# A gated linear attention feeding an expert layer: another order table for the same operations

## The chip, the cores and the metric

The kernel runs on one core of one Trainium2 chip. The metric is device time in microseconds (us), lower is better. The profiler's span, from the first to the last instruction of one execution, is a little shorter than the device time, because what lies around the program is not in it.

## The reference, cut to what matters

```
a = a * min(|a|, 0.999) / (|a| + 1e-6)            # complex a = a_re + i*a_im, per head, step, channel
for t in range(768):                              # 4 batches, 8 heads, channels of 48
    S = a[t] (*) S + outer(k[t], v[t])            # complex state 48 x 48
    y[t] = q[t] . Re(S)
x  = y with the heads side by side                # 4 x 768 x 384
xn = (x - mean(x)) / sqrt(var(x) + 1e-6) * g_ln
out = x + relu(xn @ w_ch1) @ w_ch2                # 384 -> 1536 -> 384
```

All inputs and the output are 32-bit floats. The loop over time is not run step by step. Over a chunk of 128 steps it is a masked attention: keys and queries are scaled by the running product of the decays and turned by the running phase, and a 48 x 48 state per head is carried from chunk to chunk.

## The kernel before

The 24 chunks (four batches of six) are worked in twelve pairs, P = 0 to 11; three pairs make a batch. Pair 0 alone is cut into two halves of four heads. The program is a graph of named operations with a hand-written table, PLAN, that gives the order in which they are emitted. A token such as `wl.1:G@r2.2.0` names the operation, its engine (P TensorE, V VectorE, A ScalarE, G GpSimd, S the SyncE queue that issues DMAs), for some a PSUM bank, and behind `@` an operation that it must follow. Each engine works strictly down its own list, and so does SyncE: what stands behind a waiting instruction waits too. `Graph.run` only asserts that the order is legal. What the table decides is therefore the order on each queue and, for many operations, which engine does them. Line numbers here are those of the profile of the kernel before.

One pair goes through these operations (P is the pair, n = 2P or 2P+1 the chunk):

- Loads on SyncE: `are`, `aim` (L444), `k`, `q`, `vf` (L403). A queue slot is used again only when the DMA eight issues before has landed.
- Decays, on ScalarE and VectorE: `ln` (L447), `iv` (L449), `r` = aim/are (L291), `r2`, `u` (L461), `l` (L465), `lc` (L468), then `dec` on TensorE (L476), a running sum over time, and `e`, `en` (L480), its exponentials.
- Phases: `th`, the arctangent (L484); `ph` on TensorE (L491, L495), the running sum with the carry `car` of the pair before; `sin` (L513); `qt` (L520), which adds a quarter turn in PSUM for pairs 0 to 3; `cos` (L524, L536). `tab` loads the function table for logarithms or for sines on ScalarE (L774).
- `ke`, `qe` scale keys and queries, `ks`, `qs` turn them (all L291, on VectorE or GpSimd); `v` converts the values (L413, L411).
- The turned keys and queries are needed transposed, as `ksT` and `qsT`. Either TensorE transposes them (`kT`, `qT`, L592) and VectorE or ScalarE copies the PSUM bank out (L288, L286), or one DMA transpose on SyncE does both (L597).
- `am` (L615) is scores, `atm` the mask (L291), `gm` and `G` (L643) the state, `dps` and `decc` (L572, L288) its decay, `y` (L665, L668) the output of the chunk, `x` its copy, `bn` the mean and variance, `xtr`, `xT` (L686) its transpose.
- `mm1` (L719), `relu` (L730, L732), `mm2` (L740), `ot` (L754, or `oa` and L752) and the store `st` (L760) are the feed-forward part.

Besides these, once per run: six weight loads `wl` issued by GpSimd, which convert to 16 bits on the way (L363 for `w_ch1`: wl.0 to wl.2; L365 for `w_ch2`: wl.3 to wl.5); `gln` and `wgc`, the norm's gain; `wp` (L383) and nine `wc` on VectorE (L387), which fold the gain and the mean into `w_ch1`, and which every `mm1` needs; small constants on GpSimd (`ue`, `uth`, `pick`, `ident`, `mask`, `pad`, `zdec`, `car0`, `qrow`); and fillers `warm` on TensorE (L769), multiplies whose result nobody reads.

In the order of before, GpSimd makes the constants first and issues wl.1 and wl.0 behind `r2.2.0`, wl.2 behind `qs.0.0.0` and wl.3, wl.4, wl.5 behind `v.1`. SyncE asks for the `are` and `aim` of pairs 0 to 2 first, then for `k.0.0`, `k.0.1` and `gln`, then for the rest.

Of the kernel before, what the change touches and what calls it, by code (L numbers as in the profile page):

```python
# [54 lines left out]
sin.0.0:A0 ke.0.1.0:G@lc.2.0 car.0.1:V1 sin.0.1:A1 qe.0.1.0:V qt.0.0:P0 th.2.0:A qt.0.1:P1 ph.1.0:P6
ks.0.1.1:V cos.0.0:A0 qs.0.1.1:V ks.0.0.1:V cos.0.1:A1 wp.1:P2 ks.0.0.0:V qs.0.0.1:V qs.0.0.0:V dec.2.0:P4
wc.1.0:V2 wl.2:G@qs.0.0.0 warm.69:P3 warm.70:P0 wc.1.2:V2 tab.log.2:A ln.3.0:A qs.0.1.0:G wp.0:P3 wc.1.1:V2
en.2.0:A4 ks.0.1.0:G wc.0.1:V3 qT.0:P0 iv.3.0:A wc.0.0:V3 v.0:G kT.0:P1 e.2.0:A4 wc.0.2:V3 warm.71:P2
pad.qs.1:G qsT.0:A0 qT.1:P4 ksT.0:V1 r.3.0:G vf.1.1:S kT.1:P5 qsT.1:V4 car.1.0:A6 am.0:P2 ksT.1:V5 vf.1.0:S
ph.2.0:P0 atm.0:V2 qe.1.0.1:G am.1:P4 q.2.1:S tab.trig.3:A sin.1.0:A6 ke.1.0.0:G atm.1:V4 gm.0:P2 sin.2.0:A0  # L60
are.4.0:S qt.1.0:P6 ke.1.0.1:G y.0:P3 cos.1.0:A6 qt.2.0:P0 G.0:V2 wp.2:P4 ks.1.0.1:V x.0:A3 q.2.0:S cos.2.0:A0
y.1:P5 ks.1.0.0:V xtr.0:P3 qs.1.0.1:V gm.1:P2 aim.4.0:S x.1:A5 kT.3:P6 qs.1.0.0:V th.3.0:A kT.2:P5 G.1:V2
v.1:G@qs.1.0.0 xtr.1:P7 xT.0:A3 qT.2:P0 ksT.2:V5 k.2.0:S xT.1:A7 qT.3:P1 wl.3:G ksT.3:V6 mm1.0.0.1:P2 qsT.3:V1
mm1.0.0.0:P2 r2.3.0:G qsT.2:V0 tab.log.4:A ln.4.0:A am.3:P6 wc.2.1:V4 mm1.0.1.1:P0 relu.0.0:A2 wl.4:G atm.3:V6
mm1.0.1.0:P0 u.3.0:A gm.2:P5 qe.2.0.1:G wc.2.2:V4 am.2:P2 relu.0.1:A0 ph.3.0:P6 wl.5:G wc.2.0:V4 iv.4.0:A
G.2:V5 mm1.0.2.1:P0 qe.2.0.0:G atm.2:V2 y.3:P4 r.4.0:G mm1.0.2.0:P0 car.3.0:V6 y.2:P2 x.3:V4 tab.trig.5:A
sin.3.0:A6 mm2.0.0:P3 x.2:V2 relu.0.2:A0 xtr.3:P4 qs.2.0.0:G bn.1:V qt.3.0:P6 gm.3:P5 mm2.1.0:P2 xT.3:V4
cos.3.0:A6 k.2.1:S xtr.2:P4 mm2.0.1:P3 r2.4.0:A pad.ks.2:G xT.2:V4 q.3.0:S G.3:V5 qs.2.0.1:G mm2.1.1:P2
th.4.0:A bn.3:V mm1.1.0.1:P0 vf.2.0:S bn.2:V mm1.1.2.1:P6 bn.0:V are.6.0:S rstd.1:G mm1.1.2.0:P6 tab.log.6:A
u.4.0:A l.3.0:V mm2.0.2:P3 rstd.0:G k.3.1:S relu.1.2:A6 mm1.1.0.0:P0 l.4.0:V mm1.1.1.1:P4 relu.1.0:A0 q.3.1:S  # L70
lc.3.0:V ke.2.0.1:V mm1.1.1.0:P4 ke.2.0.0:V are.5.0:S dec.3.0:P6 relu.1.1:A4 ks.2.0.1:V mm2.2.0:P0 lc.4.0:V
ks.2.0.0:V ln.6.0:A mm2.2.1:P0 k.3.0:S ot.0:V3 e.3.0:A6 mm2.2.2:P0 vf.2.1:S en.3.0:A6 qT.4:P1 qe.3.0.0:V
kT.4:P3 qe.3.0.1:V iv.6.0:A st.0:S dec.4.0:P4 qs.3.0.1:V aim.5.0:S qsT.4:A1 mm2.1.2:P2 qs.3.0.0:V ksT.4:V3
dps.3:P6 ke.3.0.1:G@qs.3.0.0 en.4.0:A4 qT.5:P7 vf.3.1:S ot.2:V0 mm2.3.0:P1 ln.5.0:A ke.3.0.0:G qsT.5:V7
q.4.0:S qT.6:P0 e.4.0:A4 decc.3:V6 ks.3.0.1:V kT.5:P3 oa.1:A2 am.4:P6 qsT.6:V0 vf.3.0:S v.2:G@ks.3.0.1
ph.4.0:P4 iv.5.0:A ksT.5:V3 ks.3.0.0:G k.4.0:S atm.4:V6 gm.4:P0 car.4.0:A4 am.5:P2 G.4:A0 aim.6.0:S mm2.3.1:P1
atm.5:V2 r.5.0:G kT.6:P0 qT.7:P6 q.4.1:S y.5:P7 tab.trig.7:A sin.4.0:A4 qsT.7:V6 kT.7:P2 ot.1:G k.4.1:S x.5:A7
y.4:P3 ksT.7:V2 th.5.0:A mm2.3.2:P1 v.3:G x.4:V3 vf.4.0:S abs.4.0:A4 dps.4:P6 ksT.6:V0 qe.4.0.0:G xtr.4:P7
am.7:P2 r2.5.0:A xT.4:V7 q.5.0:S xtr.5:P0 decc.4:V6 am.6:P4 r.6.0:G ot.3:V1 xT.5:A0 ph.5.0:P6 cos.4.0:A
vf.4.1:S atm.6:V4 mm1.2.1.1:P0 sin.5.0:A6 are.7.0:S ke.4.0.0:G atm.7:V2 y.6:P4 mm1.2.1.0:P0 abs.5.0:A6  # L80
ke.4.0.1:G gm.6:P5 x.6:A4 are.8.0:S mm1.2.2.0:P2 G.6:V5 cos.5.0:A qe.4.0.1:G xtr.6:P4 relu.2.1:V0 y.7:P6
gm.7:P5 q.5.1:S ks.4.0.1:G x.7:A6 mm1.2.2.1:P2 bn.4:V r2.6.0:A xtr.7:P0 mm1.2.0.1:P6 vf.5.0:S xT.7:V0
relu.2.2:A2 xT.6:V4 mm1.2.0.0:P6 qs.4.0.0:G G.7:V5 st.1:S th.6.0:A bn.7:V mm1.3.0.0:P0 k.5.0:S relu.2.0:V6
mm1.3.1.0:P2 ks.4.0.0:G aim.7.0:S mm1.3.2.1:P4 bn.5:V mm1.3.2.0:P4 tab.log.8:A u.5.0:A bn.6:V rstd.2:G
mm1.3.1.1:P2 u.6.0:A qs.4.0.1:V mm2.5.0:P6 l.5.0:V relu.3.2:A4 qsT.9:S mm2.4.0:P7 mm1.3.0.1:P0 lc.5.0:V
relu.3.1:A2 l.6.0:V ksT.8:S mm2.4.1:P7 ln.7.0:A relu.3.0:V0 dec.5.0:P4 vf.5.1:S mm2.4.2:P7 e.5.0:A4 q.6.1:S
lc.6.0:V v.4:V mm2.5.1:P6 en.5.0:A4 st.3:S qe.5.0.1:V dec.6.0:P2 ot.4:V7 k.5.1:S iv.7.0:A mm2.6.0:P0 en.6.0:A2
r.7.0:G k.6.1:S qT.8:P1 kT.9:P7 ln.8.0:A qsT.8:V1 mm2.5.2:P6 aim.8.0:S e.6.0:A2 ksT.9:V7 am.8:P4 qe.5.0.0:G
r2.7.0:A mm2.7.0:P1 atm.8:V4 st.4:S gm.8:P7 rstd.3:A qs.5.0.0:G st.2:S am.9:P2 u.7.0:A G.8:V7 aim.9.0:S
mm2.6.1:P0 atm.9:V2 ph.6.0:P4 ke.5.0.0:G k.6.0:S qs.5.0.1:V y.9:P2 tab.trig.9:A th.7.0:A gm.9:P7 l.7.0:V  # L90
y.8:P3 q.6.0:S mm2.7.1:P1 abs.6.0:A4 x.9:V2 ke.5.0.1:G@l.7.0 mm2.6.2:P0 are.9.0:S car.6.0:A4 G.9:V7 sin.6.0:A4
mm2.7.2:P1 x.8:V3 qe.6.0.1:V oa.6:A0 qT.11:P7 vf.6.0:S bn.8:V xtr.8:P2 xtr.9:P3 ph.7.0:P4 lc.7.0:V xT.9:A3
q.7.1:S xT.8:V2 cos.6.0:A ks.5.0.0:V mm1.4.1.1:P2 abs.7.0:V4 vf.6.1:S ke.6.0.1:G@ks.5.0.0 car.7.0:A4
mm1.4.1.0:P2 sin.7.0:A4 ks.5.0.1:V dps.6:P0 qsT.10:S oa.7:A1 v.5:V mm1.4.0.1:P4 relu.4.1:A2 ke.6.0.0:V
mm1.4.0.0:P4 qsT.11:V7 ot.6:G@ke.6.0.0 k.7.1:S kT.11:P1 relu.4.0:V4 mm1.4.2.0:P2 ks.6.0.0:G k.7.0:S
mm1.4.2.1:P2 decc.6:V0 tab.log.10:A ln.9.0:A ksT.11:V1 mm2.8.0:P7 q.7.0:S relu.4.2:A2 ot.5:V6 qe.6.0.0:G
kT.10:P0 bn.9:V am.11:P4 k.8.1:S iv.8.0:A qs.6.0.0:G mm2.9.0:P6 ksT.10:V0 rstd.4:A st.6:S dec.7.0:P2 atm.11:V4
iv.9.0:A st.5:S mm2.8.1:P7 k.8.0:S e.7.0:A2 r.8.0:V gm.10:P0 mm2.9.1:P6 en.7.0:A2 ks.6.0.1:V am.10:P4 G.10:A0
qs.6.0.1:V ksT.13:S mm2.8.2:P7 r.9.0:V qT.13:P0 mm2.9.2:P6 atm.10:V4 qsT.12:S ke.7.0.0:G@r.9.0 tab.trig.11:A
# [706 lines left out]
```

## Time and profile before

| | |
|---|---|
| Device time, median of three runs | 192.42 us (191.69 to 193.0) |
| Span of the profiled execution | 190.8 us |
| Device time of that execution | not listed by itself; the median is 1.6 us over the span |
| TensorE busy | 174.8 us |
| VectorE, ScalarE, GpSimd busy | 154.8, 157.3, 109.9 us |
| TensorE, mean granted clock | 0.987 of full speed |
| DMA transposes of `ksT`, `qsT` | 12 and 10 |
| TensorE transposes `kT`, `qT` | 12 and 14 groups of eight |
| Fillers | 72 |

How to read it: a busy share tells how long an engine had something in it, and TensorE's ends are modelled, so the share alone doesn't say that it is the bound. The timeline by engine tells when an operation started and what it waited for. The chain is the path that ended last, followed back. SPq and POOLq stand for the issuing of DMAs by SyncE and GpSimd; "to landing" is the time from a DMA's issue until its semaphore says that all of it has arrived.

### The profile page before, as it was taken

The page shows a single profiled execution, that of the slowest core. Times are in us where ns is not written, and L with a number is a line of the kernel's source. Part 1 is how long each engine was busy: PE and PEld are TensorE (multiplying, and loading weights), DVE is VectorE, ACT ScalarE, POOL GpSimd, SP SyncE. Part 2 cuts the span into 40 slices and gives each one's busy share as a digit, 9 for nine tenths or more (in the row PEclk, how much of TensorE's full clock was granted, in tenths as well). Part 3 has the DMA queues.
Part 4 walks back from the last instruction along what each step waited for, and adds up shares of the span by engine and source line. Part 5 has one row for each costly group of instructions (what it writes and reads, how often), then busy time and mean ns, then how long its engine had stood idle before and what let it go on. Part 6 is the DMA issues. An engine that isn't in the chain of part 4 may idle for free.

```text
span 190.8 us, 5173 instructions
## 1 busy us (share of the span) xinstructions
PE 174.8 (92%) x2061; PEld 134.5 (70%) x2061; DVE 154.8 (81%) x283; ACT 157.3 (82%) x217; POOL 109.9 (58%) x128
## 2 busy tenths in 40 slices
PE   5758777999999999999899999999999999999990
...
DVE  0397879998979999969979899798998898596422
...
PEclk9978999999999999999999999999999999999998
DMA  5999999899999999699989999987999999995132
GB/s 140 290 226 220 204 207 192 204 193 200 203 240 201 228 236 219 115 221 255 246 147 240 150 241 272 188 190 144 227 205 145 185 186 172 239 121 164 45 124 84
DMA packets 129768, 36.78 MB, mean 193 GB/s; under 512 B 123984, under 2 KB 129744, under 8 KB 129744
## 3 DMA queue, kind: packets, MB, share of 16 engines
...
## 4 chain that ended last, share of the span: by engine, by line
PE 50%; DMA 15%; DVE 9%; ACT 6%; POOL 6%; SPq 6%; issue 4%; POOLq 0%; DVEq 0%; ACTq 0%
PE banks L740 17%; PE banks L719 14%; DMA aim<-in_a_im_dram 5%; DMA w2b<-in_moe_w_ch_dram 4%; PE banks L592 4%; SPq L403 3%; PE banks L615 3%; PE banks L495 3%; DMA are<-in_a_re_dram 2%; PE banks L476 2%; DMA qsT<-qs 2%; DVE atm L291 2%; DMA q<-in_q_dram 2%; POOL r L291 2%; PE banks L665 2%
## 5 line engine op out<-in xcount | busy, mean ns | idle before, releaser
L740 PE MATMUL banks<-w2b,h 128*128 128x384 bf16 x288 | 55.3, 326 | 0.3 <-DMA w2b<-in_moe_w_ch_dram 0.3
L719 PE MATMUL banks<-xT,w1b 128*128 128x256 bf16 x432 | 51.3, 273 | 0.9 <-ACT trig L513 0.9
L719 PEld LDWEIGHTS <-w1b 128*128 128x128 bf16 x432 | 41.4, 98 | 7.3 <-issue 0.8
L740 PEld LDWEIGHTS <-h 128*128 128x128 bf16 x288 | 25.8, 97 | 13.5 <-issue 0.4
L291 DVE TENSOR_TENSOR atm<-banks,mask 128x1024 bf16<-128x1024 f32 x24 | 28.8, 1218 | 3.6 <-PE banks L615 3.5
L730 ACT ACTIVATE h<-banks 128x1024 bf16<-128x1024 f32 x26 | 26.0, 1019 | 5.7 <-PE banks L719 4.4
L291 POOL TENSOR_TENSOR ke<-k,en 128x384 bf16<-128x384 f32 x19 | 17.2, 916 | 16.8 <-DVE qs L291 5.8
L774 ACT ACT_TABLE_LOAD x19 | 24.4, 1283 | 1.1 <-PEq L790 0.8
L291 POOL TENSOR_TENSOR ks<-ke,trig 128x768 bf16<-128x768 bf16 (+1 forms) x12 | 18.9, 1583 | 6.6 <-DVE qs L291 2.0
L752 POOL TENSOR_TENSOR ot<-ot,x 128x384 f32<-128x384 f32 x7 | 6.4, 916 | 18.2 <-ACT ot L745 15.9
L291 POOL TENSOR_TENSOR qs<-qe,trig 128x768 bf16<-128x768 bf16 (+1 forms) x10 | 15.7, 1569 | 0.3
L754 DVE SCALAR_TENSOR_TENSOR ot<-banks,rstd,x 128x384 f32<-128x384 f32 x17 | 10.3, 610 | 6.8 <-ACT h L730 3.5
L615 PE MATMUL banks<-qsT,ksT 128*128 128x128 bf16 x192 | 14.6, 219 | 1.1 <-DVE ksT L288 0.9
L291 POOL TENSOR_TENSOR qe<-q,e 128x384 bf16<-128x384 f32 x14 | 12.7, 918 | 4.2 <-ACT trig L513 3.4
L615 PEld LDWEIGHTS <-ksT 128*128 128x128 bf16 x192 | 12.0, 98 | 3.2 <-DVE ksT L288 1.0
L291 POOL TENSOR_TENSOR r<-aim,are 128x768 f16<-128x768 f32 x6 | 10.9, 1816 | 5.5 <-ACT are L449 5.4
L476 PE MATMUL banks<-l,u_e 128*128 128x384 f16 (+1 forms) x52 | 10.9, 342 | 3.5 <-DVE l L468 3.4
L732 DVE TENSOR_SCALAR h<-banks 128x1024 bf16<-128x1024 f32 x10 | 12.1, 1216 | 2.0 <-PE banks L719 2.0
L678 DVE BATCH_NORM_STATS2 stats<-x 128x6 f32<-128x384 bf16 x24 | 13.1, 547 | 0.0
L769 PE MATMUL banks<-u_e 128*128 128x256 f16 x72 | 11.1, 312 | 2.2 <-POOL u_e L325 2.2
L447 ACT ACTIVATE w<-are 128x768 f32<-128x768 f32 (+1 forms) x13 | 10.1, 794 | 3.4 <-DMA are<-in_a_re_dram 3.3
L665 PE MATMUL banks<-v,atm 128*128 128x48 bf16 x192 | 12.1, 183 | 0.1
...
## 6 DMA issues: line engine op xcount, KB each, us to landing
...
are<-in_a_re_dram SPq DMA_DIRECT2D x11, 384.0 KB, 4.6
aim<-in_a_im_dram SPq DMA_DIRECT2D x11, 384.0 KB, 5.0
w1b<-in_moe_w_ch_dram POOLq DMA_DIRECT2D x3, 384.0 KB, 7.0
w2b<-in_moe_w_ch_dram POOLq DMA_DIRECT2D x3, 384.0 KB, 7.7
```

The source lines that it names most:

```text
L291: {"DVE": nc.vector, "POOL": nc.gpsimd}[eng(name)].tensor_tensor(**kw)
L476: nc.tensor.matmul(heads(ps[:, c]), lhsT=u_e[:, c, j], rhs=step(T("l", P), j), start=(j == 0), stop=(j == R - 1))
L615: nc.tensor.matmul(ps[:, h], lhsT=T("ksT", n)[:, h], rhs=T("qsT", n)[:, h], start=True, stop=True)
L665: nc.tensor.matmul(ps[:, h], lhsT=T("atm", n)[:, h], rhs=T("v", P)[:, c, h], start=True, stop=nfirst)
L678: nc.vector.bn_stats(out=T("stats", n), in_=T("x", n))
L719: nc.tensor.matmul(ps[:, jj], lhsT=w1b[:, dc, ts(gi * JG + jj, C)], rhs=T("xT", P)[:, dc].rearrange("p c t -> p (c t)"), start=(dc == 0), ...
L730: act(out=dst, in_=src, func=AF.Relu)
L732: nc.vector.tensor_scalar(out=dst, in0=src, scalar1=0.0, scalar2=None, op0=ALU.max)
L740: nc.tensor.matmul(bank(f"o.{n}")[:, 0:DM], lhsT=T("h", P)[:, j, ts(c, C)], rhs=w2b[:, j], start=(j == 0), stop=(j == NJ - 1))
L754: nc.vector.scalar_tensor_tensor(out=T("ot", n), in0=bank(f"o.{n}")[:, 0:DM], scalar=T("rstd", P)[:, ds(c, 1)], in1=T("x", n), op0=ALU.mul ...
L769: g.add(f"warm.{i}", lambda i=i: nc.tensor.matmul(bank(f"warm.{i}")[:, 0:256], lhsT=u_e[:, 0, 0], rhs=u_e[:, 1].rearrange("p j t -> p (j t ...
L774: g.add(f"tab.{nm}.{i}", lambda tab=tab: nc.scalar.preload_act_table_set(tab))
```

## The change

The table PLAN is replaced by another one and the number of fillers goes from 72 to 93. No operation is defined otherwise. The other line numbers shift by one.

- Weights: GpSimd issues wl.0 as its first instruction, wl.1 after seven constants, wl.2 after `r2.0.0`, `r2.0.1` and five more constants, then wl.5 and wl.4, and wl.3 a little later, all before its first `v` or `ke`.
- SyncE: the loads of pair 0's `k`, `q`, `vf` stand further back. `k.0.1` and `k.0.0` are the 14th and 15th DMA (9th and 8th before), `vf.0.0` the 23rd (17th before); `gln` is the 6th, and `vf.1.0` stands before `are.2.0`.
- Pair 0: `th` and `ph` come before `l`, `lc` and `dec`; the table loads of ScalarE are moved accordingly, 19 as before.
- VectorE: all of `ks.0` and `qs.0` and all nine `wc` come before `ksT.0`, and `r.3.0` too. Before, GpSimd did one `ke`, one `ks` and one `qs` of pair 0 and three `wc` came later.
- DMA transposes: 29 (11 `ksT`, 18 `qsT`) in place of 22. TensorE transposes: 13 `kT` and 6 `qT` in place of 12 and 14.
- Engines of other operations: `relu` 23 on ScalarE and 13 on VectorE (26 and 10 before), `v` none on VectorE (4 before), `r` 8 on GpSimd (6), `ks` 9 on GpSimd (12), and so on.
- The order of the feed-forward parts among the later pairs is another.
- Fillers: 37 before the first `ph`, 15 before `dec.0.0`, 5 around `wp.1`, 36 before `wp.2`.

The start of the two tables (about the first sixth of each; the rest differs in the same manner):

```diff
-ue:G are.0.0:S are.0.1:S aim.0.1:S uth:V are.1.0:S warm.0:P0 warm.1:P0 qrow:G@uth aim.0.0:S warm.2:P0
-warm.3:P0 pad.qs.2:G@uth warm.4:P0 aim.1.0:S warm.5:P0 zdec:G pad.ks.0:G warm.6:P0 warm.7:P0 warm.8:P0
...
-lc.0.1:V ln.2.0:A lc.0.0:V dec.0.1:P0 l.1.0:V q.1.0:S dec.0.0:P1 en.0.1:A0 warm.42:P2 warm.43:P2 iv.2.0:A
-warm.44:P4 lc.1.0:V q.0.1:S wgc:V dec.1.0:P2 en.0.0:A1 q.0.0:S r.2.0:V warm.45:P4 e.0.1:A0 warm.46:P4
-warm.47:P4 e.1.0:A2 warm.48:P4 warm.49:P4 warm.50:P4 vf.0.1:S ke.0.0.0:V e.0.0:A1 dps.1:P4 r2.2.0:V en.1.0:A2
-dps.0:P5 vf.0.0:S decc.1:V4 wl.1:G@r2.2.0 warm.51:P0 warm.52:P0 u.2.0:A decc.0:V5 warm.53:P0 warm.54:P0
-warm.55:P0 aim.3.0:S warm.56:P0 wl.0:G warm.57:P0 warm.58:P0 l.2.0:V warm.59:P0 warm.60:P0 warm.61:P0
...
+are.0.0:S tab.log.0:A ln.0.0:A iv.0.0:A are.0.1:S aim.0.1:S aim.0.0:S are.1.0:S gln:S r.0.0:V wl.0:G ln.0.1:A
+iv.0.1:A r.0.1:V ue:G uth:V one:G cmean:G vf.1.0:S wgc:V are.2.0:S car0.0:G pick:G tab.trig.1:A th.0.1:A
+aim.1.0:S zdec:G th.0.0:A warm.0:P0 warm.1:P0 warm.2:P0 warm.3:P0 warm.4:P0 warm.5:P0 warm.6:P0 warm.7:P0
...
+warm.28:P0 warm.29:P0 warm.30:P0 warm.31:P0 warm.32:P0 warm.33:P0 warm.34:P0 warm.35:P0 warm.36:P0 ph.0.1:P0
+wl.1:G aim.2.0:S r2.0.0:G@r.0.1 tab.log.2:A u.0.0:A car0.1:G ph.0.0:P1 q.1.1:S r2.0.1:G car.0.1:V0 q.0.0:S
+car.0.0:V1 l.0.0:V qrow:G wp.0:P2 vf.1.1:S ln.1.0:A wc.0.2:V2 u.0.1:A pad.qs.0:G lc.0.0:V iv.1.0:A l.0.1:V
+k.0.1:S k.0.0:S pad.ks.2:G q.0.1:S ln.2.0:A are.3.0:S wc.0.0:V2 vf.0.1:S mask:G r.1.0:V lc.0.1:V are.4.0:S
...
+en.0.1:A5 u.1.0:A wc.1.1:V4 l.1.0:V wc.0.1:V2 u.2.0:A aim.3.0:S k.1.0:S k.2.1:S warm.57:P6 warm.58:P6 warm.59:P6
...
+warm.90:P6 warm.91:P6 warm.92:P6 wp.2:P5 tab.trig.3:A th.1.0:A sin.0.0:A1 l.2.0:V lc.1.0:V ph.1.0:P2 vf.0.0:S
+sin.0.1:A0 qt.0.1:P0 ke.0.1.0:V wc.1.2:V4 ke.0.0.0:V th.2.0:A k.1.1:S wc.1.0:V4 ks.0.0.1:V ks.0.1.1:V qe.0.1.0:V
+sin.1.0:A2 qe.0.0.0:V pad.ks.0:G cos.0.1:A0 wl.5:G wl.4:G qt.0.0:P1 cos.0.0:A1 q.2.1:S dec.1.0:P6 tab.log.4:A
+e.1.0:A6 wc.2.0:V5 en.1.0:A6 lc.2.0:V qs.0.0.0:V pad.qs.1:G wc.2.1:V5 ks.0.0.0:V qs.0.1.1:V dec.2.0:P0 ln.3.0:A
+pad.ks.1:G q.1.0:S qs.0.1.0:V car.1.0:A2 ident:G dps.0:P4 ks.0.1.0:V decc.0:V4 kT.0:P6 iv.3.0:A kT.1:P4 ln.4.0:A
+qs.0.0.1:V en.2.0:A0 aim.4.0:S qT.0:P7 k.3.0:S wc.2.2:V5 wl.3:G r.3.0:V qT.1:P5 v.0:G@r.3.0 ksT.0:V6 ke.1.0.0:G
+qsT.0:V7 am.0:P6 vf.2.0:S q.2.0:S iv.4.0:A e.2.0:A0 k.2.0:S qt.1.0:P2 ke.1.0.1:G ph.2.0:P0 tab.trig.5:A
...
-    for i in range(72):
+    for i in range(93):
         g.add(f"warm.{i}", lambda i=i: nc.tensor.matmul(
```

More of the change, by code (lines that the diff above doesn't have):

```diff
@@ L55 @@
[L55 to L99, printed above, removed]
@@ new lines @@
+cos.1.0:A2 sin.2.0:A0 gm.0:P2 q.3.0:S qsT.1:V5 ksT.1:V4 am.1:P4 th.3.0:A G.0:A2 qt.2.0:P0 dps.1:P3 atm.0:V6
+qe.1.0.1:G qe.1.0.0:V ks.1.0.1:V cos.2.0:A0 qs.1.0.0:V r2.3.0:V ks.1.0.0:V decc.1:V3 ph.3.0:P6 kT.2:P3 y.0:P0
+gm.1:P2 r.4.0:G@ks.1.0.0 k.4.0:S atm.1:V4 v.1:A vf.2.1:S sin.3.0:A6 y.1:P1 x.0:V0 qs.1.0.1:V are.5.0:S
+car.3.0:A6 kT.3:P4 xtr.0:P0 qt.3.0:P6 x.1:A1 xtr.1:P1 r2.4.0:V qT.2:P5 ksT.3:V4 qT.3:P4 pad.qs.2:G are.6.0:S
+xT.0:V0 k.3.1:S xT.1:V1 mm1.0.1.1:P0 ke.2.0.0:G@r2.4.0 qe.2.0.0:G G.1:V2 th.4.0:A cos.3.0:A6 ksT.2:V3
```

133 lines of the change are left out of this document (82 added, 51 removed).

## The prediction

> **What bounds the kernel now.** I read the page's busy slices first, then the groups, then each engine's timeline over the first 50 us, then the queues. The slices show a start-up of a quarter of the span in which TensorE (PE) waits, and then a PE that is never out of work:
>
> ```profile
> PE   5758777999999999999899999999999999999990
> DVE  0397879998979999969979899798998898596422
> ...
> PEclk9978999999999999999999999999999999999998
> DMA  5999999899999999699989999987999999995132
> ```
>
> The window from the first feed-forward multiply to the last says it sharper (columns: PE, PE weight load, VectorE, ScalarE, GpSimd busy us, clock, DMA share, GB/s):
>
> ```profile
> 36.60:186.50 149.90, 147.97 (x1778) 114.28 (x1775) 128.61 (x230) 126.59 (x170) 90.42 (x85) 1.00 0.96 190
> ```
>
> PE lacks 1.9 us of 149.9, at full clock. So the time is: when that stretch begins, plus the work that PE has left, plus 4.3 us of last output, store and end. What sets the beginning is VectorE's list, and ahead of it the loads:
>
> ```profile
> 27.03 2.06 DVE L387 SCALAR_TENSOR_TENSOR w1b<-w1b,gln,banks 128x512 bf16<-128x512 bf16 x3 [0.88 <-PE banks L383]
> 29.02 0.68 DVE L288 COPY ksT<-banks 128x1024 bf16<-128x1024 bf16 x1
> 30.81 2.34 DVE L291 TENSOR_TENSOR atm<-banks,mask 128x1024 bf16<-128x1024 f32 x2
> ```
>
> The copy `ksT.0` at 29.02 frees the first scores, `am.0`, at 29.75; the first `mm1` follows at 36.64. The queue of SyncE shows what weight loads do to it. GpSimd issues two at 16.19; SyncE's next issues, normally 0.7 us, then take up to 3:
>
> ```profile
> 16.19 1.79 POOL L363 DMA_DIRECT2D w1b<-in_moe_w_ch_dram  x2 [8.63 <-DVE r L291]
> ```
> ```profile
> 15.08 1.46 SPq L403 DMA_DIRECT2D vf<-in_v_dram  x2
> ...
> 20.08 6.17 SPq L403 DMA_DIRECT2D k<-in_k_dram  x2
> 26.29 3.36 SPq L403 DMA_DIRECT2D vf<-in_v_dram  x2
> ```
>
> **The loads, step by step.** From the trace's packet records: alone, SyncE's queue moves 735 packets of 384 B per us (2 to 9 us) or 1010 of 192 B (9 to 19 us, loads only). A whole `are` or `aim` (1024 packets) so takes 1.39 us, a `k`, `q` or `vf` (1024) 1.01, `gln` 0.4. While weights run it nearly stops: from 19 to 25 us it did 1.98 us worth of its own work, from 26 to 29 us 1.07, from 38 to 48 us 3.95. The weight packets that ran in these stretches make 1.86, 0.96 and 2.98 loads, so one weight load costs the queue 2.0 to 2.2 us; I take 2.05. Check on the kernel before, first packets at 2.0: `vf.0.0` comes out at 20.8 (landed 20.96), `k.1.1` at 29.8 (30.56), `vf.2.0` at 46.8 (49.58). So the sum is right to 0.2 to 2.8 us, never too late.
>
> GpSimd in the new order: wl.0 at 0.8; `ue` to `zdec` as in the old timeline to 5.4; wl.1; then it waits for `r.0.1`. That needs `aim.0.0`, 2.8 of queue work plus one weight load plus 2.0, and 1.5 which the early loads lag behind my sum in the old trace (`aim.0.0` 6.2 by the sum, 7.75 landed): 8.3, and `r.0.1` ends near 9.3. Two halves of `r2` (0.75 each, half of the 1.48 row) and constants (0.4 to 0.9) put wl.2 at 14 us, wl.5 and wl.4 at 15.5 and 16.3, wl.3 at 19. Packets start 2 us after an issue in the old trace, so from 16 to 27 us four weight loads run end to end. By 16 us the queue has done about 9.5 us of its work. `k.0.0` needs 6 x 1.39 + 0.4 + 6 x 1.01 = 14.8. All six weight loads are ahead of it: 2.0 + 14.8 + 6 x 2.05 = 29.1, with half a microsecond of lag 29.6. The old order had it at 11.0, because its weights were asked for at 16 us and later. `aim.3.0` lands at 35.3, `vf.0.0` at 38.3 by the same sum.
>
> **VectorE.** Its list reaches `ke.0.1.0` about 24 us (`aim.2.0` lands near 18.5; then `r.2.0` 0.9, `r2` 0.5, two `wc` 1.3, two `l` 1.8, `lc` 0.35). That needs `k.0.1` and `k.0.0`, and everything for `ksT.0` stands behind it: it stands until 29.6. Then, by start-to-start times in the old timeline: two `ke` 0.92, five `wc` 3.35, eight `ks`, `qs` 2.24, two `qe` 1.12, `lc` 0.35, `decc` 0.38, `r.3.0` 0.88, `ksT.0` 0.60, `qsT.0` 0.68, in all 10.5. So `am.0` at 40.1 in place of 29.75. From there to `xT.1`: two copies 1.2, two `atm` 2.26, `qe` 0.56, four `ks`, `qs` 1.88, two `r2` 0.96, `decc` 0.38, `x` 0.5, `ksT.3` 0.6, two `xT` 0.7, in all 9.0. First `mm1` at 49.1, 12.5 later than at 36.6.
>
> **PE.** Seven groups of transposes go from PE to the DMA queue. One costs PE 0.45 (first of these lines of the chain of waits; the second is four `mm2`): 7 x 0.45 = 3.15 less. `ph.3.0` (0.97) and `qt.3.0` (0.32) now lie ahead of the first `mm1`, in waiting time: 1.3 less behind it.
>
> ```profile
> 63.89 0.45 PE banks L592 x8
> 64.74 0.65 PE banks L740 x4
> ```
>
> Fillers: 21 more, 0.11 to 0.21 each, all ahead of `wp.2`. The first 37 end near 9 to 11 us, beside `th.0.1`, which waits for `r.0.1`; the 36 run from about 18.5 to 23, beside wl.2's landing (14 + 7). They cost nothing unless the waits they cover vanish, then at most 21 x 0.21 = 4.4. After them PE stands idle from about 25 to 34 us. In the old trace an idle of 3.6 us before 11.77 was followed by this clock (third number from the end):
>
> ```profile
> 13.40:15.40 2.00, 2.00 (x10) 1.09 (x8) 1.76 (x5) 1.42 (x4) 0.00 (x0) 0.51 1.21 286
> ```
>
> Half clock for some 3.4 us, while VectorE is the bound: 0.5 on the path (bounds 0 and 1.7).
>
> DMA transposes: seven more. A packet of them takes 28.5 ns on average and one transpose has 64 per DMA engine: 1.8 us of DMA each, 12.8 in all; SyncE takes 1.44 us (median) to issue one, 10 in all. SyncE stood waiting for others about 13 us between 50 and 172, so I take 0. Bounds: 0, and 7 x 0.42 = 2.9, the one stall of PE that a transpose caused (before `am.22`, at 171.8). Other changes of engine: VectorE's durations add up to the same within 0.3, ScalarE has 7 less, GpSimd 2 more, none of them the bound behind 49 us; 0, bounds -1.9 (PE's whole idle time) and +2.
>
> **Sum.** 190.8 + 12.5 - 1.3 - 3.15 + 0.5 = 199.4 of span, +1.6 for what lies around it (the median, 192.42, less the profiled span): 201.0.
>
> **Rivals.**
>
> *Cheap weights.* The weight loads share the DMA engines rather than stop the queue. At the best row of bytes (300 GB/s from 5 to 8 us) 384 KB take 1.3 us, six 7.9: `k.0.0` at 25.2, `am.0` at 35.7, first `mm1` at 44.7, +8.1, so 196.6. For it: no row shows weights at the very start. Against it: three stretches with the same 2 us. The Trainium skill, "DMA: Bandwidth & Descriptors", section "Anatomy of one DMA — SWDGE (gpsimd) path", fits such a DMA as 2.0 us plus bytes over 436 GB/s, an estimate of 0.9 us of moving per load and 195.4 in this sum; the trace has 5.8 to 9.0 us to landing where that fit gives 2.9.
>
> ```profile
> w1b<-in_moe_w_ch_dram POOLq DMA_DIRECT2D x3, 384.0 KB, 7.0
> ```
>
> *The table keeps its promise (faster).* If `k.0` lands before VectorE arrives and that list runs dense, 22.5 us of work from 7.9 on, `am.0` is near 30.4; if PE's dense stretch then begins as early as before, only the 3.15 us less of its work count: 189.3. It decides at a first `mm1` before 39.2 (36.6 + 1.3 + 3.15 - 1.9). Against it: VectorE would have to wait for neither `gln`, `aim.2.0` nor `k.0.0`.
>
> *Same.* First `mm1` between 39.2 and 43.0: 190.5 to 194.3.
>
> *SyncE becomes the bound.* 29 transposes, 1.44 us each at the queue, can't use its waits; late `qsT` stall PE repeatedly. Half of the 12.8 us shows: 207.
>
> **How the numbers follow.** Forecast 0.54 (own range 197 to 205: lag of 0 to 2.8, transposes up to 2.9), cheap weights 0.17, SyncE 0.10, same 0.09, faster 0.10. A change under 1% can't be told from none here (three runs span 0.7%). So slower 0.81, same 0.09, faster 0.10. The range goes from 192.5 to 207.5: below it the faster case and a little of "same", above it half of the SyncE case.
>
> **What would show it.** Right: `k.0.0` lands near 29.6, VectorE idle before `ke.0.1.0` with the `k` load as releaser, first `mm1` near 49, PE dense behind it, 19 groups of transposes. Wrong: `ke.0.1.0` at 24 without a wait (weights cheap), PE gaps behind 60 us released by a `qsT` DMA (SyncE), or a first `mm1` before 39.

## The result and the profile after

| | before | after |
|---|---|---|
| Device time, median of four runs | 192.17 us (191.69 to 193.0) | 203.7 us (203.0 to 204.27) |
| Ratio to before | 1 | 1.060, 95% interval 1.056 to 1.065 |
| Span of the profiled execution | 190.8 us | 202.2 us (its device time 203.99) |
| TensorE busy | 174.8 us | 175.8 us |
| VectorE, ScalarE, GpSimd busy | 154.8, 157.3, 109.9 us | 157.5, 152.0, 112.5 us |
| First `mm1` (start of its weight load on TensorE) | 36.59 us | 50.81 us |

Line numbers of the new kernel are one lower than those of the kernel before (`mm1` is L718, `ot` L753, the loads L402 and L443). The busy slices of the new kernel:

```profile
PE   2947920799999999999999999999999999999690
...
DVE  0059806999999999998899999999959859906552
...
PEclk9999985579999999999999999999999999999997
DMA  5999998998999999999999999998999899680124
```

TensorE is busy for good only from the ninth slice on, 40 us; its hole is the sixth and seventh, 25 to 35 us, and the clock is at half in the seventh and eighth. The DMA row shows no pause in it: the chip is loading all that time, but not what TensorE waits for. From the first to the last feed-forward multiply TensorE is nearly as full as it was, 2.5 us short of 143.0 (columns as in the prediction):

```profile
50.90:193.90 143.00, 140.49 (x1697) 109.27 (x1695) 123.82 (x218) 116.25 (x158) 91.68 (x84) 1.00 0.93 191
```

So again the time is the beginning of this stretch, plus the work left, plus the end. By the starts of TensorE's weight loads, of which none is missing from the trace, the span grew like this: the first `mm1` comes 14.2 us later; the work behind it is 4.45 us less (140.44 for 144.89, a nominal time for each operation summed over the list); the idle time in that stretch is 0.5 more (5.0 for 4.5); from the first weight load of the last `mm2` to the end it is 1.1 more (6.4 for 5.3). Together 11.4, which is 202.2 less 190.8.

What holds the beginning up, on VectorE's timeline:

```profile
24.44 0.35 DVE L467 TENSOR_SCALAR l<-l 128x768 f16<-128x768 f16 x1
31.86 0.56 DVE L290 TENSOR_TENSOR ke<-k,en 128x384 bf16<-128x384 f32 x1 [7.07 <-DMA k<-in_k_dram]
...
40.88 0.68 DVE L287 COPY ksT<-banks 128x1024 bf16<-128x1024 bf16 x1
```

VectorE is done with the decays at 24.8 and stands for 7.07 us, the bracket says for whom: the load of `k`. `ksT.0` follows at 40.88; it was at 29.02. GpSimd's issues, and the rows of the six loads (KB of one, and the median us from issue to landing of three, in the last two columns):

```profile
1.30 0.99 POOL L362 DMA_DIRECT2D w1b<-in_moe_w_ch_dram  x1 [0.80 <-POOLq L789]
5.25 0.80 POOL L362 DMA_DIRECT2D w1b<-in_moe_w_ch_dram  x1
15.17 0.80 POOL L362 DMA_DIRECT2D w1b<-in_moe_w_ch_dram  x1
16.44 1.52 POOL L364 DMA_DIRECT2D w2b<-in_moe_w_ch_dram  x2
19.55 0.76 POOL L364 DMA_DIRECT2D w2b<-in_moe_w_ch_dram  x1
```
```profile
w1b<-in_moe_w_ch_dram POOLq DMA_DIRECT2D x3, 384.0 KB, 7.4
w2b<-in_moe_w_ch_dram POOLq DMA_DIRECT2D x3, 384.0 KB, 10.7
```

And SyncE's issues at the same time, where `k.0.1` and `k.0.0` take 6.40 us together and the next `q` 4.25:

```profile
17.55 6.40 SPq L402 DMA_DIRECT2D k<-in_k_dram  x2
23.99 4.25 SPq L402 DMA_DIRECT2D q<-in_q_dram  x1
28.35 2.48 SPq L443 DMA_DIRECT2D are<-in_a_re_dram  x1
```

`k.0.0` lands at 31.76. The next lines show the other place where time went, the end. VectorE waits three times for a store to give back one of the three `ot` buffers, and TensorE waits behind the first of them for its PSUM bank (where its results stand until VectorE has read them):

```profile
190.71 0.62 DVE L753 SCALAR_TENSOR_TENSOR ot<-banks,rstd,x 128x384 f32<-128x384 f32 x1 [2.03 <-DMA out_dram<-ot]
...
195.53 0.62 DVE L753 SCALAR_TENSOR_TENSOR ot<-banks,rstd,x 128x384 f32<-128x384 f32 x1 [1.42 <-DMA out_dram<-ot]
198.18 1.14 DVE L753 SCALAR_TENSOR_TENSOR ot<-banks,rstd,x 128x384 f32<-128x384 f32 x2 [2.03 <-DMA out_dram<-ot]
```
```profile
191.38 1.47 PE L718 MATMUL banks<-xT,w1b 128*128 128x256 bf16 x12 [1.70 <-DVE ot L753]
```

### The profile page after: what moved, and what is told of

Same layout as the page of the kernel before. It is cut to its first block, busy times and chain, and to the rows that moved or that the text cites. A ratio compares the mean times of both kernels' runs of the same rounds, so it can differ in the third digit from the quotient of the medians.

```text
span 202.2 us, 5113 instructions
## 1 busy us (share of the span) xinstructions
PE 175.8 (87%) x2024; PEld 135.2 (67%) x2026; DVE 157.5 (78%) x284; ACT 152.0 (75%) x208; POOL 112.5 (56%) x130
## 4 chain that ended last, share of the span: by engine, by line
PE 55%; DVE 13%; DMA 11%; SPq 10%; POOL 4%; issue 2%; ACT 2%; DVEq 0%; POOLq 0%
PE banks L718 18%; PE banks L739 16%; DMA out_dram<-ot 6%; DMA k<-in_k_dram 6%; PE banks L614 5%; SPq L402 4%; SPq L443 4%; PE banks L591 3%; PE banks L494 2%; PE banks L664 2%; PE banks L475 2%; DVE atm L290 2%; PE banks L667 2%; SPq L366 2%; PE banks L685 2%
## 5 line engine op out<-in xcount | busy, mean ns | idle before, releaser
L718 PE MATMUL banks<-xT,w1b 128*128 128x256 bf16 x432 | 52.2, 272 | 2.0 <-DVE ot L753 1.7
L718 PEld LDWEIGHTS <-w1b 128*128 128x128 bf16 x432 | 41.2, 98 | 8.2 <-issue 2.3
L729 ACT ACTIVATE h<-banks 128x1024 bf16<-128x1024 f32 x23 | 23.2, 1020 | 7.9 <-PE banks L718 7.5
L412 POOL TENSOR_SCALAR v<-vf 128x768 bf16<-128x768 f32 x9 | 8.3, 921 | 27.9 <-DVE r L290 20.8
L290 POOL TENSOR_TENSOR ks<-ke,trig 128x768 bf16<-128x768 bf16 x9 | 14.7, 1639 | 12.5 <-PE banks L718 8.2
L475 PE MATMUL banks<-l,u_e 128*128 128x384 f16 (+1 forms) x52 | 10.6, 328 | 11.4 <-DVE l L467 11.4
L290 POOL TENSOR_TENSOR qs<-qe,trig 128x768 bf16<-128x768 bf16 x9 | 14.7, 1642 | 5.6 <-ACT h L729 2.4
L290 POOL TENSOR_TENSOR ke<-k,en 128x384 bf16<-128x384 f32 x17 | 15.5, 914 | 3.6 <-DVE l L464 1.7
L768 PE MATMUL banks<-u_e 128*128 128x256 f16 x93 | 13.2, 307 | 3.7 <-POOL u_e L324 3.7
L290 POOL TENSOR_TENSOR r<-aim,are 128x768 f16<-128x768 f32 x8 | 14.5, 1813 | 2.5 <-ACT trig L523 2.5
L731 DVE TENSOR_SCALAR h<-banks 128x1024 bf16<-128x1024 f32 x13 | 15.6, 1215 | 0.1
L475 PEld LDWEIGHTS <-u_e 128*128 128x128 f16 x52 | 5.0, 100 | 14.9 <-DVE l L467 10.3
L753 DVE SCALAR_TENSOR_TENSOR ot<-banks,rstd,x 128x384 f32<-128x384 f32 x16 | 9.5, 610 | 6.9 <-DMA out_dram<-ot 6.0
L768 PEld LDWEIGHTS <-u_e 128*128 128x128 f16 x93 | 10.2, 110 | 5.9 <-POOL u_e L324 3.4
## 6 DMA issues: line engine op xcount, KB each, us to landing
w2b<-in_moe_w_ch_dram POOLq DMA_DIRECT2D x3, 384.0 KB, 10.7
```

The costliest lines, as they stand in the source:

```text
L290: {"DVE": nc.vector, "POOL": nc.gpsimd}[eng(name)].tensor_tensor(**kw)
L412: {"DVE": nc.vector, "POOL": nc.gpsimd}[eng(nm)].tensor_scalar(out=T("v", P), in0=T("vf", P), scalar1=1.0, scalar2=0.0, op0=ALU.mult, op1= ...
L475: nc.tensor.matmul(heads(ps[:, c]), lhsT=u_e[:, c, j], rhs=step(T("l", P), j), start=(j == 0), stop=(j == R - 1))
L718: nc.tensor.matmul(ps[:, jj], lhsT=w1b[:, dc, ts(gi * JG + jj, C)], rhs=T("xT", P)[:, dc].rearrange("p c t -> p (c t)"), start=(dc == 0), ...
L729: act(out=dst, in_=src, func=AF.Relu)
L731: nc.vector.tensor_scalar(out=dst, in0=src, scalar1=0.0, scalar2=None, op0=ALU.max)
```

## The experiments

The theory was that of the prediction: each weight load asked for ahead of the first pair's loads keeps SyncE's queue from about 2 us of its own work, all that matters to VectorE and TensorE waits behind that, and the rest of the new table costs nothing. The rivals: the new order of SyncE's list or of VectorE's, the DMA transposes, the fillers, the end. The kernels ran in three groups, each on another chip and beside the kernel before on the same chip (e1 to e4, e5 to e8, e9 to e12); its medians were 191.54, 191.94 and 191.68 us. "First `mm1`" and "idle behind it" are taken from TensorE's weight loads as above (before 36.59 and 4.5, after 50.81 and 5.0), from the one profiled execution of each run.

| run | time, us | ratio to before, 95% | first `mm1` | idle behind it |
|---|---|---|---|---|
| e1_w2b_late | 205.38 | 1.062 to 1.078 | 47.5 | 9.5 |
| e2_k0_first | 207.82 | 1.076 to 1.092 | 54.9 | 5.4 |
| e3_old_weights_at_once | 205.73 | 1.064 to 1.080 | 51.0 | 4.1 |
| e4_old_29_transposes | 196.87 | 1.016 to 1.032 | 35.6 | 13.7 |
| e5_new_ring6 | 200.46 | 1.040 to 1.048 | 51.0 | 3.4 |
| e6_w2b_spread | 204.41 | 1.058 to 1.070 | 43.1 | 11.6 |
| e7_old_w2b_early | 198.68 | 1.032 to 1.043 | 42.6 | 4.2 |
| e8_old_ring6 | 192.23 | 0.997 to 1.004 | 36.0 | 5.2 |
| e9_new_57_fillers | 200.76 | 1.039 to 1.054 | 49.1 | 4.6 |
| e10_new_22_transposes | 212.36 | 1.096 to 1.112 | 49.1 | 12.6 |
| e11_new_no_weights | 195.65 | 1.013 to 1.025 | 43.4 | 4.7 |
| e12_old_no_weights | 195.00 | 1.007 to 1.022 | 41.4 | 4.0 |

### The weights alone, in the old table: e3

```diff
-  wl.1:G@r2.2.0  wl.0:G  wl.2:G@qs.0.0.0  wl.3:G  wl.4:G  wl.5:G      (at 16 to 41 us)
+  wl.0:G first, wl.1:G behind zdec, wl.2:G wl.5:G wl.4:G wl.3:G behind pad.qs.0
```

> The old table, with only the six weight loads moved to where the new one has them in time: wl.0 first on GpSimd, wl.1 behind zdec, wl.2, wl.5, wl.4, wl.3 behind the last early constant. Theory: all six run before about 22 us, so the loads of 14 to 30 us land about 9 to 12 us later (q.0.0 near 29 in place of 17.7, aim.3.0 near 35 in place of 26.4); VectorE stands at a qe of pair 0 or 1, the first mm1 comes 8 to 11 us later than 36.6, and the time is 200 to 203. Rival (the order of the other operations is what costs, not the weights): within 2 us of the kernel before, 190 to 194.

Measured 205.73, and the first `mm1` at 51.03, 14.4 us later than in the old table. Where it waits:

```profile
27.00 0.68 DVE L374 TENSOR_SCALAR gc<-cmean,gln 128x128 bf16<-128x128 f32 x3 [7.36 <-DMA gln<-in_moe_g_ln_dram]
```
```profile
15.55 6.77 SPq L367 DMA_DIRECT2D gln<-in_moe_g_ln_dram  x1
```

A tiny load, `gln`, needs 6.77 us on SyncE's queue only to be issued, because the queue in front of it does not drain, and `wgc` waits 7.36 us for it. One part of the change, moved alone into a table in which nothing else was changed, costs all that the whole change costs, and 2 us more. The theory stands; its size was too small here (+14 for +8 to +11). The dose is not quite that of the new kernel: wl.0 and wl.1 are issued at the same times, but the other four at 9.8 to 12.1 us instead of 15.2 to 19.6, because GpSimd does not wait for `r.0.1` in between.

### Half the dose: e7

```diff
-  ... v.1 wl.3:G r2.3.0 wl.4:G qe.2.0.1 wl.5:G
+  pad.qs.0:G wl.5:G wl.4:G wl.3:G        (w1b's three loads stay)
```

> The old table with only w2b's three loads moved early (behind pad.qs.0 on GpSimd, at about 8 us), w1b where it was. Theory (each weight load ahead of the first pair costs its loads 2.2 to 2.4 us of the DMA engines' time): first mm1 at 36.6 + 7 = 43.6, time 192 + 7 = 199. Rival 1 (w1b at once was what cost, w2b finds free time early): 192 to 194. Rival 2 (the three stand in front of w1b on the GpSimd queue, so the first pair's matmuls wait for w1b as well as for its own loads): first mm1 beyond 46, time 202 or more.

Measured 198.68, first `mm1` at 42.6 (+6.0). SyncE's issues in this run, and the same issues in the kernel before:

```profile
11.28 4.20 SPq L444 DMA_DIRECT2D are<-in_a_re_dram  x1
15.53 5.97 SPq L403 DMA_DIRECT2D q<-in_q_dram  x3
```
```profile
10.75 0.49 SPq L444 DMA_DIRECT2D are<-in_a_re_dram  x1
11.29 3.75 SPq L403 DMA_DIRECT2D q<-in_q_dram  x3
```

`k.0.1`, `gln` and `aim.2.0` land 5.7, 7.0 and 6.5 us later (17.37, 18.95, 20.37 for 11.67, 11.92, 13.90): 1.9 to 2.3 us for each of three weight loads. Three cost a little under half of what six cost (6.0 for 14.4 us at the first `mm1`). Rival 1 falls, and there is no sign of rival 2.

### What the price is made of

The trace's packet records of the new kernel, packets begun in each microsecond from 21 to 29:

```
GpSimd's queue, 768 B   180  186  189  181  190  192  192   84
SyncE's queue,  192 B   223  216  194  184  195  188  190  818
```

In this stretch they go one to one, a packet of 768 B against a packet of 192 B, about 190 of each per us; alone, SyncE's queue does about 1000 of 192 B. A `w2b` load is 512 such packets: it lasts 512 / 190 = 2.7 us, in which SyncE's queue does 512 of its own, 0.5 us worth. So one costs that queue 2.2 us. The 768 B are what is written, after the conversion; by the kernel's own shapes 1536 B are read for them. One to one is not the rule everywhere: in the two microseconds from 4 to 6, where `w1b`'s packets of 1024 B ran against packets of 384 B and SyncE had three loads open, it was 107 and 144 against 37 and 107. The Trainium skill, "DMA: Bandwidth & Descriptors", section "Queues, rings and completion order", says that each DMA engine "round-robins between the queue rows it has work for, at *packet* granularity". That the two queues take turns agrees with these records; but that page's packet is a group of about 9 to 17 descriptors, and whether a record here is such a group or a part of one no run shows. The fit on the same page, section "Anatomy of one DMA — SWDGE (gpsimd) path", which the rival "cheap weights" used, gives an estimate of 2.9 us for such a load by itself; here, beside a busy second queue and in part behind other loads of their own queue, the medians were 7.4 (`w1b`) and 10.7 (`w2b`).

### The later half moved behind the first pair, in the new table: e1 and e6

```diff
 e1:  wl.2:G ...                     v.0:G@r.3.0
-     wl.5:G wl.4:G ... wl.3:G
+     ... v.0:G@r.3.0  wl.3:G wl.4:G wl.5:G
```

> The new table, with only the three loads of w_ch2 (wl.3, wl.4, wl.5) issued later by GpSimd, behind v.0. Theory (weights asked for at once starve the loads of SyncE, and k.0.0 holds VectorE): each weight load out of the way gives k.0.0 back 2.2 us, so it lands near 25.2 in place of 31.8, ke.0.1.0 starts as soon as VectorE arrives (24.8 to 25.5), am.0 near 35.5, the first mm1 near 44.5 in place of 50.8, and the time falls by 5.5 to 6.5 us to about 197.5. Rival 1 (the place of k.0 in the queue of SyncE, 14th and 15th, is what makes it late): k.0.0 moves by less than 2 us and the time by less than 2. Rival 2 (VectorE's longer list in front of ksT.0 is what counts): no change, within 1 us.

Measured 205.38, no gain. The first half of the theory held in part: `k.0.0` landed at 26.43, VectorE, which came to it at 26.52, did not wait, and the first `mm1` came at 47.5, 3.3 us earlier where 6.3 had been expected. Then it was given back: idle time behind the first `mm1` went from 5.0 to 9.5.

```profile
39.58 5.01 SPq L404 DMA_DIRECT2D k<-in_k_dram  x1
44.69 4.03 SPq L404 DMA_DIRECT2D q<-in_q_dram  x1
```
```profile
54.06 0.56 DVE L292 TENSOR_TENSOR qs<-qe,trig 128x768 bf16<-128x768 bf16 x1 [3.73 <-POOL qe L292]
```

The weights, now issued at 36 to 38 us, kept pair 2's `k` and `q` from the queue (`k.2.0` landed at 50.36, 48.77 in the new table, though TensorE was now 3.3 us ahead), GpSimd waited 4.5 us for it ahead of `ke.2` and `qe.2`, VectorE for those, and `dec.3.0` on TensorE for VectorE. So e6 let pair 2 go ahead and spread the three loads:

```diff
+  q.2.0:S k.2.0:S ahead of aim.4.0:S;  k.3.0:S behind vf.2.0:S
+  wl.3:G behind qe.1.0.1, wl.4:G behind ke.2.0.0, wl.5:G behind qe.2.0.1
```

> The new table with w1b's three loads where they are, w2b's three spread over the first pairs (behind qe.1.0.1, ke.2.0.0 and qe.2.0.1 on GpSimd) and q.2.0 and k.2.0 asked for ahead of them. Theory (what stands ahead of a load in the queues decides, and the late w2b of the earlier experiment cost its gain only because pair 2 stood behind it): first mm1 at 47.5 as there, am.0 at 36, the idle time behind the first mm1 back from 9.5 to about 5 us, span 198.7, time about 200.4. Rival (the sum of the loads up to 55 us is the bound, whichever is put first): another load starves in its turn and the time stays at 203 to 206.

Measured 204.41: the rival. The first `mm1` comes at 43.1, 7.7 us earlier than in the new table, and idle time behind it is 11.6 us. Pair 2 is on time (`k.2.0` landed at 37.12), and now pair 3's keys and the decays of pair 6 are late (`k.3.1` landed at 54.39, `are.6.0` at 51.49):

```profile
51.58 0.84 ACT L449 ACTIVATE w<-are 128x768 f32<-128x768 f32 x1 [2.54 <-DMA are<-in_a_re_dram]
54.52 0.92 POOL L293 TENSOR_TENSOR ke<-k,en 128x384 bf16<-128x384 f32 x1 [2.45 <-DMA k<-in_k_dram]
```
```profile
64.13 0.62 PE L594 MATMUL banks<-ident,ks 128*128 128x128 bf16 x8 [1.21 <-POOL ks L293]
```

So in both runs moving three of the loads moved who pays: what the table then lacks is not one load's place but SyncE's queue time for all of them, somewhere before 55 us. All six at the places of the old table, with the new order of everything else, were not tried. Of the 4.4 us between the first `mm1` of e1 and that of e6, 2.8 are not the change: `r.0.0`, ahead of which the two tables are the same, started at 11.11 in e1 and at 8.36 in e6 (more on this under e9).

### Pair 0's keys ahead of the other loads: e2

```diff
+  gln:S k.0.1:S k.0.0:S q.0.1:S q.0.0:S vf.1.0:S are.2.0:S aim.1.0:S ...
```

> The new table, with only the loads k.0.1, k.0.0, q.0.1, q.0.0 of SyncE moved forward, behind gln; the weights stay where they are. Theory (whatever stands in SyncE's queue behind the weights starves): k.0.0 lands near 15, but aim.2.0 now has four loads more ahead of it and falls into the stretch of four weight loads, landing near 27 to 31 in place of 17.6; VectorE then stands at r.2.0, which is ahead of ke.0.1.0, and nothing is won: the time goes from 3 us faster to 6 us slower, about +3. Rival 1 (the place of k.0 is the cause): VectorE finds k.0 there, the 7.1 us wait before ke.0.1.0 is gone with nothing in its place, and the time falls by 5 to 7 us.

Measured 207.82, first `mm1` at 54.9: 4 us worse. Rival 1 falls. With the keys ahead, `are` and `aim` of pairs 1 and 2 come later (`aim.1.0` lands at 26.67 and `aim.2.0` at 31.04, 16.14 and 17.61 in the new kernel), and VectorE needs their decays before `am.0` as well (`dec.1.0` at 36.9 in place of 25.8, `r.2.0` of VectorE only at 31.2). Its waits for `aim` (us in total, times, longest; the longest is that for the very first load):

```profile
DVE r L292 <- DMA aim<-in_a_im_dram: 20.8, 3, 10.2
```

The place of pair 0's keys in SyncE's list is not what cost; other orders of that list were not tried.

### No weights at all: e11 and e12

```diff
-  nc.gpsimd.dma_start(out=w1b[...], in_=moe_w_ch1...)     and the same for w2b
+  nc.vector.memset(w1b[:, :, ts(i, 512)], 0.03)           wl.0 to wl.5 first on VectorE
```

> The new table with no weight loads at all: w1b and w2b are filled with constants by VectorE at the start, so the weights are left out of the result and the loads of the first pairs have the DMA engines to themselves. Theory (six loads at 2.2 us stand in the way of k.0.0): it lands 12 to 13 us earlier, at about 19, first mm1 at 38 to 40; behind it the idle time is 10 to 12 us as in the run with w2b spread, since the other engines then set the pace; time 196 to 199. Rival 1 (the loads are all that is wrong with the table): idle time 5 us as in the new table, time 190 to 192. Rival 2 (the first pairs are bound by the order of the other engines by now): first mm1 no earlier than the 43.1 of the run with w2b spread, time 202 to 204.

> The old table with no weight loads, w1b and w2b filled with constants by VectorE behind uth, so the weights are left out of the result. It is the measure for the new table without them: what then remains between the two is the order alone. Theory (in the old table the weights' loads lie beside other work, the first mm1 is set by VectorE's chain): 0 to 2 us less than 192, first mm1 at 35 to 36.6. Rival (aim.3.0, which lands at 26.35 behind w1b, holds the old table too): 3 to 5 us less, 187 to 189.

Measured 195.65 and 195.00: without the weights the two tables take about the same time. (Their output is not that of the reference, since the weights are constants; the runs serve for times alone.) Both are held up by their own fill: six fills of 1.34 us on VectorE end at 10.55 in the new table and at 12.12 in the old, so that `r.0.0` starts at 10.46, 4.4 us after `aim.0.0` landed (6.08), in the new, and at 12.04 in place of 7.88 in the old. In the old table the first `mm1` moved by a little more than that 4.2 us (41.4 for 36.6), so by this run the weights had hardly cost it anything where they were; my "0 to 2 us less" missed because of the fill. In the new one `k.0.0` lands at 16.63, VectorE runs from 10.46 to `ksT.0` at 33.31 with no wait for a load, and the first `mm1` is at 43.4. Behind it:

```profile
43.50:186.50 143.00, 140.71 (x1699) 109.44 (x1697) 123.89 (x218) 116.48 (x158) 91.32 (x84) 1.00 0.93 187
```

This window is cut to the length of that of the new table. From the first `mm1` to the start of the last `mm2` the run takes 144.7 us, 145.0 in the new table, though it begins 7.4 us earlier, and idle time is 4.7. That is rival 1 for the idle time, and it settles e6: with the same first `mm1` (43.1 and 43.4) the run with spread weights lost 11.6 us and the run without weights 4.7, so the loads and not the other engines' lists caused the loss. What the order alone is worth between these two runs: 4.45 us of TensorE's work less behind the first `mm1`, 2.0 us later to get there (43.4 against 41.4), 0.7 us more idle time behind it and 1.4 us more at the end (6.4 against 5.0): 0.3 us less in all, the difference of the two spans (194.5 and 194.8). The 2.0 us are rather more by the order itself, since the fill ends earlier in the new table: from `r.0.0` to the first `mm1` it is 33.0 us against 29.4.

### The DMA transposes: e4 and e10

```diff
 e4, old table:  - qT.8 qsT.8:V  qT.11 qsT.11:V  ... kT.12 ksT.12:A    (seven groups)
                 + qsT.8:S  qsT.11:S  qsT.13:S  qsT.14:S  qsT.15:S  qsT.16:S  ksT.12:S
 e10, new table: the other way round, copies on VectorE
```

> The old table with only seven more of the transposes of ksT and qsT done by DMA (qsT.8, 11, 13, 14, 15, 16 and ksT.12), 29 in all as in the new table, each issued beside the other DMA transpose of its pair. Theory (TensorE is the bound after the start and SyncE's queue has room): 7 groups of 0.45 us go from TensorE, the time falls by 1.5 to 3.2 us, to 189 to 190.7. Rival (29 transposes make SyncE's queue the bound): TensorE waits for qsT or for late loads, and the time rises by 2 to 8 us.

Measured 196.87, slower than the old table: TensorE's work is 3.15 less, idle time behind the first `mm1` 13.7 for 4.5. The largest piece:

```profile
101.77 1.01 PE L614 MATMUL banks<-qsT,ksT 128*128 128x128 bf16 x8 [3.72 <-DMA qsT<-qs]
```

`qsT.11` was issued at 98.11, behind `qsT.10`, and landed 3.6 us later, and the old list of TensorE has nothing to put in between. The rest is spread in pieces of at most 1.2 us.

> The new table with the seven groups of transposes that it gave to DMA back on TensorE, their copies on VectorE (22 DMA transposes left, as in the old table). Theory (in this order the DMA transposes are covered, so the 3.15 us of TensorE's work that they save is really saved): TensorE's work back by 3.15, idle time behind the first mm1 as before, time 206.9. Rival 1 (they cost as much in waits as they save, as in the old table): 203 to 204. Rival 2 (VectorE, 97% busy from 50 to 90 us, pays for seven more copies of about 0.65 us as well): 208 to 211.

Measured 212.36, beyond rival 2. TensorE's work grew by 3.15 and idle time from 5.0 to 12.6, with VectorE as the releaser:

```profile
119.23 1.46 PE L742 MATMUL banks<-w2b,h 128*128 128x384 bf16 x8 [1.45 <-DVE ksT L290]
126.54 0.81 PE L721 MATMUL banks<-xT,w1b 128*128 128x256 bf16 x6 [0.84 <-DVE qsT L290]
```

With this placement taking the seven groups back costs more than the 3.15 us of TensorE's work, because VectorE gets seven copies as well. What the DMA transposes are worth in the new order is not settled: I put each copy on VectorE directly behind its transposes, where VectorE, in strict order, also waits for them; a better place may cost less.

### The ring of result tiles: e5 and e8

```diff
-  "ot": 3
+  "ot": 6
```

> The new table with six buffers instead of three for the result tiles ot. Theory (the end is bound by the ring: VectorE's last ot steps wait for a store to free one of three buffers, 1.86 us of it seen by TensorE at mm1.11.2.0 and 1.2 us behind the last matmul): both go, the span falls by 2 to 3 us, to 199.2 to 200.2, the time to about 200.9. Rival (the stores themselves are the pace at the end, so the wait only moves from the ring to the last store): within 0.7 us of 203.7.

> The old table with six buffers instead of three for the result tiles ot. Theory (here the end does not wait for the ring as it does in the new table: 4.3 us behind the last matmul): 0 to 1.2 us less, 190.4 to 191.6. Rival (the ring is as much of a bound here): 2 to 3 us less, 189.

The new table 200.46, 3.2 us less; the old one 192.23, no difference. In the new table with six buffers no `ot` waits for a store any more, the last two wait only for TensorE:

```profile
188.60 1.12 DVE L755 SCALAR_TENSOR_TENSOR ot<-banks,rstd,x 128x384 f32<-128x384 f32 x2
...
194.96 1.14 DVE L755 SCALAR_TENSOR_TENSOR ot<-banks,rstd,x 128x384 f32<-128x384 f32 x2 [1.25 <-PE banks L741]
```

Idle time behind the first `mm1` falls from 5.0 to 3.4, and from the first weight load of the last `mm2` to the end it is 4.5 for 6.4. The wait did not move to the stores. The new table's order of the last `ot` needs more than three buffers, the old order does not.

### The fillers: e9

```diff
-  warm.57 ... warm.92 ahead of wp.2
```

> The new table without the 36 fillers ahead of wp.2 (57 left). Theory (as the prediction had it, fillers lie in TensorE's wait for the first loads and cost or bring nothing): within 0.8 us of the new table's 203.7, first mm1 within 0.4 of 50.8. Rival (they hold the clock up for wp.2 and the phases behind it): wp.2, ph.1.0 and what follows run at a lower clock and the first mm1 is 0.5 to 2 us later.

Measured 200.76, 2.9 us less than the new kernel, where theory and rival had both expected no less. But the difference lies where these fillers do not stand. The first waits of VectorE, in this run, in e10 (same chip, all 93 fillers) and in the new kernel:

```profile
8.28 1.03 DVE L289 TENSOR_TENSOR r<-aim,are 128x384 f16<-128x384 f32 x2 [8.28 <-DMA aim<-in_a_im_dram]
```
```profile
8.76 1.03 DVE L293 TENSOR_TENSOR r<-aim,are 128x384 f16<-128x384 f32 x2 [8.76 <-DMA aim<-in_a_im_dram]
```
```profile
9.66 1.03 DVE L290 TENSOR_TENSOR r<-aim,are 128x384 f16<-128x384 f32 x2 [9.66 <-DMA aim<-in_a_im_dram]
```

The very first loads land 0.9 to 1.4 us earlier in e9 and e10, long before the fillers in question, which begin at 19.8. `k.0.0` lands at 30.01 and 30.10 there, at 31.76 and 31.99 in the new kernel and in e5, and the first `mm1` is at 49.1 in e9 and e10, at 50.8 and 51.0 in the other two. So 1.7 us are found with all the fillers too. In the profiled executions, 198.4 and 202.2, another 1.6 is the end (4.8 for 6.4): the middle one of the three waits for an `ot` buffer is missing, because the store `st.21` lands 1.9 us after its issue in e9, 3.6 in the new kernel. That is so in e10 as well (1.9).

Neither goes with the chip. Up to what `r.0.0` needs, the lists of SyncE and GpSimd are the same in the new kernel and in e1, e2, e5, e6, e9 and e10, and `r.0.0` started at 9.66, 11.11, 10.15, 9.64, 8.36, 8.28 and 8.76: e1 and e2 ran on one chip, e5 and e6 on another. In the kernel before and in e4, e7 and e8, where no weight load is asked for that early, it was 7.58 to 7.88. The scatter was seen only with a weight load at the start; what sets it from run to run stays open.

What the fillers do change is seen: without the 36, `wp.2` starts at 19.89, in e10 at 22.86, and the clock is at half from 23.9 to 27.4 us as well, as the rival had it; VectorE still waits 6.65 us for `k`, 7.07 in the new kernel. An effect of the fillers on the time beyond that scatter was not shown, and with it none under 2 us can be excluded.

## Why the prediction was right, point by point

In span the forecast was 2.8 us short, 199.4 for 202.2: 1.7 us at the first `mm1` (50.8 for 49.1) and 1.1 at the end. The 0.5 for the clock did not come, and 0.5 of idle time that was not forecast stands in its place, which is luck.

- *The loads.* Right in kind, a little low in size. `k.0.0` at 31.76 for 29.6, `aim.3.0` at 37.37 for 35.3, `vf.0.0` at 40.04 for 38.3: all about 2 us late. Put into the prediction's own sum, 31.76 makes one weight load 2.4 us, not 2.05; e7 has 1.9 to 2.3 and e10, where `k.0.0` landed at 30.10, 2.1. The mis-sized term is 6 times 0.1 to 0.35, and the scatter seen under e9 is as large. That the term exists and makes up the change, e3 and e7 showed in the old table, and e11, where `k.0.0` landed at 16.63, in the new one.
- *VectorE.* It arrived at `ke.0.1.0` at 24.8 (24). From there, 9.9 us to `am.0` (10.5) and 9.1 to the first `mm1` (9.0). The two sums of rows were right to 0.6 us.
- *TensorE.* 4.45 us less behind the first `mm1`, as the sum had it (3.15 and 1.3). TensorE did come back at half clock, and for longer than forecast: the clock's row has two fives around 35 us, and in the trace's clock records half clock lasts from 28.9 to 42.6 us, 13.7 us, where the sum had some 3.4. But with VectorE's own sum from 31.86 the first `mm1` is at 51.4 and it came at 50.8, so the 0.5 does not show as a term of its own.
- *DMA transposes at nothing.* Right in the new table: no gap of TensorE in it is released by a `qsT` or `ksT` DMA. It was right because of the order, not because such a DMA is free: e4 paid 9.2 us of idle time for seven that the new table gives to the DMA queue too.
- *Fillers at nothing.* Nothing against it, and not shown to better than 2 us.
- *The end, 4.3 us unchanged.* This step failed. The `ot` ring costs 1.9 us of idle time within the last multiplies (1.70 in the row of `mm1` above, 1.9 counted by its weight loads), and the end behind them is 1.1 longer than before; e5 got 3.2 us back. I had costed the end at the old rows without looking at the order of the last `ot` and `st` in the new table, which the diff shows. It was partly hidden in the total, because the idle time elsewhere in the stretch was 1.4 less.
- *The rivals.* "Cheap weights" needed `k.0.0` at 25.2 and the first `mm1` at 44.7; they came at 31.76 and 50.8. "The table keeps its promise" needed a first `mm1` before 39.2 and it came at 50.8; without any weights it came at 43.4, with a fill of up to 4.4 us in the way, so at 39.0 at best, the edge of that rival's condition. "SyncE becomes the bound" was seen only in the old order, in e4.

No version here beats the kernel before. The best of the new table that loads its weights is that with the larger ring, 200.46 (e9's 200.76 may be the scatter told of above); the ring together with the spread weights was not tried, and by their parts (204.41 less 3.2) it would be about 201.
